# Half of the first product of blocks 1 and 2 as Strassen steps, with weight quarters combined on GpSimd

## The chip, the cores and the metric

The kernel runs on one core of one Trainium2 chip. The metric is the device time of one execution in microseconds. TensorE is called PE, VectorE DVE, ScalarE ACT, GpSimd POOL and SyncE SP; "PEld" is PE's loading of weights, which overlaps its matmuls.

## The reference

Attention within chunks of 64 tokens, for 8 heads of 64 columns, and behind it a gated two-layer product over 4608 tokens:

```python
scores = (1/8) * q_c @ k_c.T            # each chunk of 64 tokens, each head
x = (softmax(scores) @ v_c)             # laid out as 4608 tokens x 512
h = x @ w_in                            # 512 -> 2048
g = h * clip(h + 3, 0, 6) / 6
out = g @ w_out                         # 2048 -> 512
```

## The kernel before, in words

**Blocks.** The tokens go as 9 blocks of 512 (`NBLK`, L25). Block n has two halves of 4 heads, called heads n0 and n1. For each, `Attention` (L205 to L329) runs scores (PE), maximum, subtraction, exponential, sum, division, a transpose and a product with v on PE, and leaves the half block's x in SBUF, for blocks 0 to 2 as a high and a low part (`keep`, `rest`, L312 to L325). PE's tile `two` is one, so the scores of a half wait for the `rest` of the half before.

**Numbers in two parts.** Every f32 product is three matmuls with 128x128 weights and 512 columns: high by high, high by low, low by high (`passes`, L334 to L338). A high part is a cast on ACT, the low part a subtraction on DVE.

**Block 0** is a plain two-layer product while the weights are still coming in and being converted (16 column groups `ft` of w_in and 16 row groups of w_out, 8 tiles each, called a0 to a7 and b0 to b7).

**Blocks 1 and 2.** Their first product is plain too: for each block all 16 `ft` (`mm`, L618), 4 x 3 matmuls each (`mm1_half`, L340), then `relu` (ACT) and `gate` (DVE) into the b tiles (L701 to L714). Their second product is a Strassen product: 7 half-size products in place of 8 (`second_product`, L896).

**Blocks 3 to 8** go in three pairs. The pair is one 2x2 problem and both of its products take seven half-size products per group of columns. In `first_product` (L797) that is, for each of 8 groups p, f1, f5, f6, f7, f2, f3, f4 (`ORDER_A`), 6 matmuls each, and on DVE the sums u2, u4, s7, s3, s4 and four gates (L835 to L851); f2, f3 and f4 accumulate into a bank of an earlier one after its sum was taken, so f3 waits for u4 and f4 for s7. On POOL two subtractions of gates, t1 and t2 (L853, L855). For blocks 1 and 2 t1 and t2 are on DVE (L867, L869).

**Weight sums.** Strassen's products need sums of the quarters of w_in and w_out. For each of 8 groups of either weight (`sum_steps`, L418) `whole` makes a full copy, on DVE (L433) or by a transfer (L430); `combine` (L435 to L438) makes four sums of 128x256 in place, on DVE; `high` and `lower` split them (L443, L446) into one of two `hl` tiles; `send` and `send_own` write them to DRAM (L451, L457), from where the later products fetch them. The groups u = 0 to 7 are of w_out, 8 to 15 of w_in (L755 to L766).

**Slots.** The second product of blocks 1 and 2 needs space: 8 slots, the tiles a0 to a7 of w_in, of which 3 take fetched weights and 5 the split operands (`next_slot`, L489; casts and subtractions L884, L887). Before, slot k is free once the plain product of block 2 with ft 2k+1 is done (L501).

**Order.** All steps are handed to `Schedule` (L52), which knows an engine, a fixed cost, predecessors and a due time for each, and writes one order per engine. Each engine then runs its list in order; a waiting step holds up all behind it on its engine. The cost table is fixed in the code and does not know of two engines getting in each other's way. `PLACES` (L600) names the PE steps behind which a half block's last product, merged with the scores of the next half, is put.

Of the kernel before, what the change touches and what calls it, by code (L numbers as in the profile page):

```python
# [18 lines left out]
P = 128  # L19
# [12 lines left out]
NFP = NFT // 2  # L32
ORDER_A = (1, 5, 6, 7, 2, 3, 4)
# [6 lines left out]
ROWS = []  # L40
# [8 lines left out]
SECOND = STEP * 33  # L49
# [70 lines left out]
def tile_kernel(ctx: ExitStack, tc: tile.TileContext, qk_in, v_in, weights, out):  # L120
# [7 lines left out]
    raw = pool("raw", NDP)  # L128
# [9 lines left out]
    xp = std.enter_context(tc.tile_pool(name="xp", bufs=NDP))  # L138
# [66 lines left out]
    class Attention:  # L205
# [106 lines left out]
        def keep(self):  # L312
            if self.n >= NHI:
                if self.n not in xraw:
                    xraw[self.n] = raw.tile([P, NDP, 2, NT], F32, name="x")
# [101 lines left out]

    def sum_steps(m, p):  # L418
# [16 lines left out]
        def combine():  # L435
            for to, x, y, op in ((q(1, 1), q(1, 0), q(1, 1), ALU.add), (q(1, 0), q(0, 0), q(1, 0), ALU.subtract),
                                 (q(0, 0), q(1, 1), q(0, 0), ALU.subtract), (q(0, 1), q(0, 1), q(0, 0), ALU.subtract)):
                DVE.tensor_tensor(out=to, in0=x, in1=y, op=op)  # L438

        def high():  # L440
            t["hl"] = hp.tile([P, 2, 2, 2, 256], F32R, name="hl")
            t["s"] = t["a"].rearrange("p f (k t) -> p f k t", k=2)
            ACT.copy(out=t["hl"][:, :, :, 0], in_=t["s"])  # L443
# [45 lines left out]
    def next_slot(s, name, until, stream=False):  # L489

        if s == 0:
            first, n = (0, RING) if stream else (RING, NFP - RING)
            k = first + slots[stream] % n
# [8 lines left out]
        return k, before  # L502

# [31 lines left out]


# [4 lines left out]
    spare = {"qk01": lambda: xp.tile([P, 2, NB, 2 * CH], F32, name="x"),  # L541
# [6 lines left out]
    def attention(u, due, scores=(), less=(), keep=(), bank=None):  # L548
# [10 lines left out]
        if u in ROWS:  # L559
            rows = [("negate", "DVE", 0.12, a.negate, ()), *[(f"exp{k}_", "ACT", 2.3, lambda k=k: a.exps(k, e() if k == 0 else None), less if k == 0 else ()) for k in range(4)],  # L560
                    ("invert", "DVE", 0.45, a.invert, ())]
        steps = [("scores", "PE", 1.30, a.scores, ["qk" + u, *scores]), ("max", "DVE", 1.23, a.largest, ()), *rows, ("share", "DVE", 1.22, a.share, ()), ("turn", "PE", 1.07, a.turn, ()),
                 ("turned", "ACT", 1.02, a.turned, ()), ("product", "PE", 2.26 if after else 1.50, products if after else a.product,
                  ["v" + u, *(["qk" + after, *[x for _ in HALF for x in work.take(*RINGS[bank], "product" + u, [made[u]])]] if after else [])]),
# [28 lines left out]
    due_of = {"10": 13 * STEP, "11": 15 * STEP, "20": 20.5 * STEP, "21": 24 * STEP}  # L593
    for s in range(1, NSUP):
        n = NSTD + 2 * s
        for k, u in enumerate((f"{n}0", f"{n + 1}0", f"{n + 1}1", f"{n}1")):
            chain.append(u)
            due_of[u] = STEP * (28, 35.5, 39.3, 42)[k] if s == 1 else START[s - 1] + PART * (30, 51, 73, 94)[k]
    prior = dict(zip(chain[1:], chain))
    PLACES = {"21": ("a", NFT + 14), "30": ("a", NFT + 22), "40": ("s", 0, 1), "41": ("s", 0, 3), "31": ("s", 0, 6)}  # L600
# [21 lines left out]
    def place(u, bank=None):  # L622
        n = int(u[0])
        s = (n - NSTD) // 2
        free = () if n == 1 else [f"b{NFT - 1}"] if n == 2 else [f"b{2 * NFT - 1}"] if s == 1 else [f"x{s - 1}.{i}l" for i in ORDER_A]
        attention(u, due_of[u], [made[prior[u]]] if u != "10" else ["b0"], ["product" + prior[u]], free, bank)
# [74 lines left out]
    for j, (n, ft) in enumerate(mm):  # L701
        first, second, relu, gate, high, lower, sums, send, bank, under = tile_steps(n, ft)
        of = lambda name, back: f"{name}{j - back}" if j >= back else None
        at = STEP * j if n == 0 else STEP * (NFT + 1) + STEP / 2 * (j - NFT)
        apart = j < APART
        before = [] if apart and j % 2 else [of("b", 1)]
        work.add(f"a{j}", "PE", PART * 2 / 3 if apart else PART, [f"{'high' if apart else 'lower'}a{ft // 2}" if n == 0 else None, *before, made[f"{n}0"], *work.take("o" if spare_bank(j) else "h", 4 if spare_bank(j) else 2, f"a{j}", [f"gate{j}"])], first, due=at)
        if apart:
            work.add(f"l{j}", "PE", PART / 3, [f"a{j}", f"lowera{ft // 2}"], under, due=at)
        work.add(f"b{j}", "PE", PART, [f"l{j}" if apart else f"a{j}", of("b", 1), made[f"{n}1"]], second, due=at + PART)  # L710
        if n:
            place_at(("a", j), bank_o)
            add_relu_gate(f"{j}", f"b{j}", bank, lambda n=n, ft=ft: gate_of(ft // NFP, n - 1, ft % NFP), at + STEP, [f"{s}{ft // 2 * 2 % d + k}" for s, d in (("own", NFP), ("c", NFT), *([] if in_dram(1, ft // 2 * 2 % NFP) else [("whole", NFP)])) for k in range(2)])
# [83 lines left out]
    def first_product(s):  # L797
        work.add(f"lay{s}", "none", 0.0, [f"ul{s - 1}.{i}.{k}" for i in ORDER_B for k in range(NFP // 2)], lambda: None)
        before = f"s{s - 1}.{SLOTS - 1}"
        g = GRAIN[s]  # L800
        ceil = lambda n: (n + g - 1) // g
        for p in range(NFP):
            t = {}
            gq = lambda r, c, p=p: gate_of(r, c, p)
            id_ = lambda name, p=p: f"{name}{s}.{p}"
            feeds = [add_fetch(s) for _ in range(ceil(4) + ceil(3))]
            for k, i in enumerate(ORDER_A):
                name = id_(f"f{i}.")
# [25 lines left out]
                new = lambda key, t=t: lambda: keep_tile(t, key, lambda: tp.tile([P, NT], F32, name=key))  # L834
                if i == 1:  # L835
                    work.add(id_("p1."), "ACT", 0.59, [name, f"lay{s}", *work.take("p1", 2, id_("p1."), [id_("u2.")])],
                             lambda o=new("p1"), x=of(1): ACT.copy(out=o(), in_=x()), due=due)
                elif i == 6:
                    work.add(id_("u2."), "DVE", 0.69, [name, id_("p1."), *work.take("u2", 2, id_("u2."), [id_("s3."), id_("s4.")])],
                             add(new("u2"), of(6), of("p1")), due=due)  # L840
                    work.add(id_("u4."), "DVE", 0.69, [id_("f5."), id_("u2."), *work.take("u4", 2, id_("u4."), [id_("s7.")])],
                             add(new("u4"), of(5), of("u2")), due=due)
                elif i == 7:
                    work.add(id_("s7."), "DVE", 0.69, [name, id_("u4.")], add(of(6), of(7), of("u4")), due=due)
                    add_relu_gate(id_("7."), id_("s7."), of(6), lambda f=gq: f(1, 1), due)
                elif i == 2:
                    add_relu_gate(id_("2."), name, of(1), lambda f=gq: f(0, 0), due)
                elif i in (3, 4):
                    out = (lambda f=gq: f(0, 1)) if i == 3 else (lambda f=gq: f(1, 0))
                    work.add(id_(f"s{i}."), "DVE", 0.69, [name, id_("u2.")], add(of(j), of(j), of("u2")), due=due)  # L850
                    add_relu_gate(id_(f"{i}."), id_(f"s{i}."), of(j), out, due)  # L851
                    if i == 3:
# [43 lines left out]
    def second_product(s):  # L896
# [15 lines left out]
        before = f"f{ORDER_A[-1]}.{s}.{NFP - 1}" if s else f"b{len(mm) - 1}"  # L912
# [114 lines left out]
```

## Time and profile before

| | |
|---|---|
| median of 3 runs | 786.94 us (786.46 to 787.82) |
| span of the profiled execution | 784.5 us |
| PE busy | 776.5 us (99%) |
| DVE busy | 634.5 us (81%) |
| ACT busy | 377.4 us (48%) |
| POOL busy | 71.4 us (9%) |
| granted PE clock | 0.999 of full speed |

The span is what the profiler saw from the first to the last instruction. The profiled execution's own time is not among the three runs listed; the median lies 2.44 us above its span, which is what lies around it. Busy shares of engines that overlap do not add up; what matters is which of them something waits for, stretch by stretch.

The stretches by their borders in the trace: block 0 until about 146 us, mixed with block 1 from about 101 us; block 2's plain product 167 to 213.5 us; second product of blocks 1 and 2 213.5 to 299.2 us; then the pairs.

### The profile page before, as it was taken

What the parts mean: (1) busy time and instruction counts of PE and PEld (TensorE: products, weight loads), DVE (VectorE), ACT (ScalarE), POOL (GpSimd) and SP (SyncE); (2) the same over time, 40 slices, a digit from 0 to 9 for tenths busy, and PEclk for the clock granted to TensorE, in tenths of its full rate; (3) what the DMA queues carried; (4) which work ended last, traced back from release to release, by engine and by line L of the source; (5) the groups of instructions that cost most, each with busy time, mean ns of one, the idle gap of its engine ahead of it and who ended that gap; (6) DMA issues with size and microseconds to landing.
All of it is one profiled execution on the core that took longest, in us unless ns stands there. A gap on an engine that the chain in (4) does not pass through costs nothing.

```text
span 784.5 us, 13920 instructions
## 1 busy us (share of the span) xinstructions
PE 776.5 (99%) x5625; PEld 639.6 (82%) x5627; DVE 634.5 (81%) x780; ACT 377.4 (48%) x461; POOL 71.4 (9%) x55
## 2 busy tenths in 40 slices
PE   7999999999999999999999999999999999999998
PEld 4788888888888888888888888888888888888887
DVE  6998998898899988968998687678988657679841
ACT  4998743445554454344644433436543423355330
POOL 0000000000000001322200003231100013222000
PEclk9999999999999999999999999999999999999999
DMA  9999996879779696556676785577666665666572
GB/s 370 408 412 329 353 370 228 280 257 331 288 237 343 215 364 224 195 187 248 203 251 239 248 278 196 197 246 245 197 200 218 217 200 195 202 199 207 197 236 90
DMA packets 69424, 198.05 MB, mean 252 GB/s; under 512 B 7024, under 2 KB 19568, under 8 KB 65008
## 3 DMA queue, kind: packets, MB, share of 16 engines
q1 hardware_dynamic: 69216, 197.03, 72.7%
q8 instruction: 44, 0.72, 0.4%
q14 instruction: 20, 0.16, 0.1%
q10 hardware_dynamic: 144, 0.13, 0.0%
HBM read 153.09 MB, written 44.04 MB: 251 GB/s over the span
## 4 chain that ended last, share of the span: by engine, by line
PE 97%; DMA 1%; DVE 1%; ACT 0%; issue 0%; SPq 0%; ACTq 0%
PE acc L336 22%; PE acc L338 21%; PE acc L337 21%; PE h L336 9%; PE h L338 9%; PE h L337 9%; PE two L228 2%; PE two L278 2%; PE h L304 1%; DMA x<-qk_in 1%; PE two L304 1%; PE acc L304 0%; PE h L352 0%; DVE z L246 0%; DVE m L235 0%; DVE e L266 0%
## 5 line engine op out<-in xcount | busy, mean ns | idle before, releaser
L336 PE MATMUL acc<-wa,ws 128*128 128x512 f32 (+1 forms) x536 | 209.2, 390 | 0.0
L338 PE MATMUL acc<-wa,ws 128*128 128x512 f32 (+1 forms) x536 | 207.8, 388 | 0.0
L337 PE MATMUL acc<-wa,ws 128*128 128x512 f32 (+1 forms) x536 | 207.8, 388 | 0.0
L884 ACT CAST wa<-wb 128x1024 fp32r<-128x1024 f32 x96 | 100.4, 1052 | 110.4 <-PE acc L338 66.2
L887 DVE TENSOR_TENSOR wa<-wb,wa 128x1024 fp32r<-128x1024 f32 x96 | 124.0, 1300 | 26.1 <-ACT wa L884 25.4
L336 PEld LDWEIGHTS acc<-wa,ws 128*128 128x128 f32 x536 | 100.6, 188 | 20.7 <-DVE u L789 0.3
L338 PEld LDWEIGHTS acc<-wa,ws 128*128 128x128 f32 x536 | 100.6, 188 | 20.7
L337 PEld LDWEIGHTS acc<-wa,ws 128*128 128x128 f32 x536 | 100.7, 188 | 20.1
L853 POOL TENSOR_TENSOR wb<-wb 128x512 f32<-128x512 f32 x24 | 31.9, 1330 | 637.6 <-DVE wb L682 624.2
L679 ACT ACTIVATE r<-acc,half 128x512 f32<-128x512 f32 x86 | 58.4, 685 | 51.1 <-DVE acc L789 34.0
L679 ACT ACTIVATE r<-h,half 128x512 f32<-128x512 f32 x42 | 28.9, 688 | 108.8 <-DVE h L789 89.8
L682 DVE SCALAR_TENSOR_TENSOR wb<-r,acc 128x512 f32<-128x512 f32 x86 | 58.0, 679 | 8.4 <-ACT r L679 8.2
L338 PE MATMUL h<-wa,ws 128*128 128x512 f32 (+1 forms) x144 | 55.2, 383 | 0.0
L337 PE MATMUL h<-wa,ws 128*128 128x512 f32 (+1 forms) x144 | 55.2, 383 | 0.0
L336 PE MATMUL h<-wa,ws 128*128 128x512 f32 (+1 forms) x144 | 55.2, 383 | 0.0
L336 PE MATMUL h<-x,wa 128*128 128x512 f32 x132 | 52.2, 396 | 0.0
L338 PE MATMUL h<-x,wa 128*128 128x512 f32 x132 | 51.5, 390 | 0.0
L337 PE MATMUL h<-x,wa 128*128 128x512 f32 x132 | 51.4, 390 | 0.0
L789 DVE TENSOR_TENSOR u<-h,p 128x512 f32<-128x512 f32 x32 | 21.9, 688 | 27.7 <-PE h L338 27.5
L789 DVE TENSOR_TENSOR acc<-acc,u 128x512 f32<-128x512 f32 x48 | 32.8, 695 | 9.6 <-PE acc L338 9.6
L682 DVE SCALAR_TENSOR_TENSOR wb<-r,h 128x512 f32<-128x512 f32 x42 | 28.6, 682 | 14.1 <-ACT r L679 14.0
L855 POOL TENSOR_TENSOR g<-wb,wb 128x512 f32<-128x512 f32 x24 | 38.7, 1613 | 1.9
(116 smaller groups left out, 1299.0 us busy)
## 6 DMA issues: line engine op xcount, KB each, us to landing
ws<-b SPq DMA_DIRECT2D x84, 512.0 KB, 4.6
ws<-a SPq DMA_DIRECT2D x72, 512.0 KB, 4.2
qk<-qk_in SPq DMA_DIRECT2D x17, 1024.0 KB, 7.5
wa<-b SPq DMA_DIRECT2D x28, 512.0 KB, 6.3
a<-wa SPq DMA_DIRECT2D x40, 256.0 KB, 6.1
v<-v_in SPq DMA_DIRECT2D x17, 512.0 KB, 5.4
wa<-w_in_out SPq DMA_DIRECT2D x8, 1024.0 KB, 12.2
wb<-w_in_out SPq DMA_DIRECT2D x8, 1024.0 KB, 11.2
```

Source lines behind the costliest of these rows:

```text
L228: PE.matmul(self.s[o, a, c, :], lhsT=self.qk[rows, 0, c, o], rhs=self.qk[rows, 1, c, o], start=True, stop=True)
L278: PE.transpose(out=self.tp[:, a, i], in_=self.e[:, a, 2 * i:2 * i + 2].rearrange("p c t -> p (c t)"), identity=ident)
L336: PE.matmul(ps, lhsT=a_h, rhs=b_h, start=first, stop=False, skip_group_check=more)
L337: PE.matmul(ps, lhsT=a_h, rhs=b_l, start=False, stop=False, skip_group_check=more)
L338: PE.matmul(ps, lhsT=a_l, rhs=b_h, start=False, stop=last, skip_group_check=more)
L679: ACT.activation(out=t["r"], in_=ps(), func=AF.Relu, bias=half, scale=1.0 / 6.0)
L682: work.add("gate" + name, "DVE", 0.69, ["relu" + name, *more], lambda: DVE.scalar_tensor_tensor(out=out(), in0=t["r"], scalar=1.0, in1=ps( ...
L789: return lambda: DVE.tensor_tensor(out=out(), in0=x(), in1=y(), op=ALU.add)
L853: work.add(id_("t1."), "POOL", 1.45, [id_("gate3."), id_("gate2.")], lambda f=gq: POOL.tensor_tensor(out=f(0, 1), in0=f(0, 1), in1=f(0, 0) ...
L855: work.add(id_("t2."), "POOL", 1.45, [id_("t1."), id_("gate7.")], lambda f=gq, p=p: POOL.tensor_tensor(out=t2_of(p), in0=f(1, 1), in1=f(0, ...
L884: ACT.copy(out=g_ops[s, i, pp][:, :, 0], in_=src())
L887: work.add(low, "DVE", 1.22, [high], lambda i=i, pp=pp, src=src: DVE.tensor_tensor(out=g_ops[s, i, pp][:, :, 1], in0=src(), in1=g_ops[s, i ...
```

## The change

Of the 16 `ft` of blocks 1 and 2's plain first product, 8 stay plain (0, 1, 8, 9, 2, 3, 10, 11, which are p = 0 to 3). The other 8 (p = 4 to 7) go through `first_product(0)`: seven half-size products for each p. They take the sums of w_in from the `hl` tiles in SBUF (`parked`) and the plain quarters from the a tiles, so nothing is fetched for them. Sums and splits of x are new steps (`first_x_steps`): two taken from the attention's PSUM banks and one more on DVE, four on POOL, four casts on ACT, four subtractions on DVE; they use the last row groups of w_out's tiles (b3, b7) and the tiles a0, a4, a1, a5. All 16 `combine` go to POOL, and so do t1 and t2 of blocks 1 and 2. The sums of w_in for p = 4 to 7 come ahead of those for p = 0 to 3, which move into the second product's stretch. Slots are freed by the new products. The halves 40 and 41 take their exponentials as 16 pieces on ACT, with sums, instead of one exponential on ACT and a subtraction and a sum on DVE. Block 2's attention is due four steps of 5.448 us earlier; blocks 3 and 4's halves go in the order 30, 31, 40, 41. Buffers for x are renamed (not shown).

```diff
+NPL = 4
+PLAIN = [p + q + NFP * r for p in range(0, NPL, 2) for r in range(2) for q in range(2)]
+FIRST = {0: list(range(NFT)), 1: PLAIN, 2: PLAIN}
+HELD = {5: 0, 6: 4, 7: 1, 4: 5}
...
-ROWS = []
+ROWS = ["40", "41"]
+XDVE = ["x0.s0c"]
...
-SECOND = STEP * 33
+SECOND = STEP * (17 + 2 * NPL) + PART * 7 * (NFP - NPL)
+STEPS = SECOND - PART * 7 * (NFP - NPL)
+COMBS = [u for u in range(16)]
...
-        def combine():
+        def combine(engine):
...
-                DVE.tensor_tensor(out=to, in0=x, in1=y, op=op)
+                engine.tensor_tensor(out=to, in0=x, in1=y, op=op)
...
-            before = [f"b{2 * NFT + 2 * k + 1}", *[f"{step}{NFP + (2 * k + q) % NFP}" for step in ("own",) for q in range(2)]]
+            before = [f"f4.0.{2 * (k % 4) + 1}", *owns(k)]
...
+        work.add("x0.s0", "DVE", 1.22, ["product20", "rest10", "c7", "own6", "own7"], from_banks("20", 5, x(1, 0, 0)), due=due_of["20"])
+        work.add("x0.s1", "DVE", 1.38, ["product21", "x0.s0c"], from_banks("21", 6, of(5)), due=due_of["21"])
...
+            on = name not in XDVE
+            work.add(name, "POOL" if on else "DVE", 2.7 if on else 1.22, after, op(POOL if on else DVE, i, one, two, kind))
...
+            work.add(f"x0.{i}h", "ACT", 1.05, [last, f"b{2 * NFT + 2 * k + 1}", *owns(k)], lambda i=i: high(i))
+            work.add(f"x0.{i}l", "DVE", 1.22, [f"x0.{i}h"], lambda i=i: lower(i))
...
+        if i in (1, 2, 4):
+            return w_of(0, p + NFP * (i == 4))[:, :, 256 * (i != 1):256 * (i != 1) + 256]
+        row, col = {5: (1, 1), 7: (1, 0), 6: (0, 0), 3: (0, 1)}[i]
+        return parked[0, p][:, row, col]
...
-    PLACES = {"21": ("a", NFT + 14), "30": ("a", NFT + 22), "40": ("s", 0, 1), "41": ("s", 0, 3), "31": ("s", 0, 6)}
+    PLACES = {"21": ("a", NFT + 10), "30": ("f", 0, 4), "31": ("s", 0, 0), "40": ("s", 0, 2), "41": ("s", 0, 4)}
...
-    mm = [(n, ft) for n in range(NHI) for ft in range(NFT)]
+    mm = [(n, ft) for n in range(NHI) for ft in FIRST[n]]
...
-    for u in range(2 * NFP):
+    for u in [*range(NFP), *range(NFP + NPL, 2 * NFP), *range(NFP, NFP + NPL)]:
...
-        due = SECOND + (4 * (u - 7) if u < NFP else -35 + 5.5 * (u - 8))
+        due = STEPS - 8 + 4 * (u - 7) if u < NFP else STEPS - 3 + PART * 7 * (p - NPL) if p >= NPL else SECOND + 10 + 12 * p
+        last = [f"f3.0.{p}"] if u >= NFP + NPL else []
...
-        work.add(f"comb{u}", "DVE", 1.70, [f"whole{u}"], combine)
-        work.add(f"top{u}", "ACT", 1.05, [f"comb{u}", *work.take("hl", 2, f"top{u}", [f"send{u}"])], high)
+        work.add(f"comb{u}", *(("POOL", 3.2, [f"whole{u}"], lambda f=combine: f(POOL)) if u in COMBS else ("DVE", 1.70, [f"whole{u}"], lambda f=combine: f(DVE))))
+        work.add(f"top{u}", "ACT", 1.05, [f"comb{u}", *work.take("hl", 2, f"top{u}", [f"send{u}", *last])], high)
...
+    SLOT_OF = (2, 0, 5, 6, 4, 1, 3, 7)
...
-        for p in range(NFP):
+        for p in range(0 if s else NPL, NFP):
...
-                work.add(f"t1.0.{p}", "DVE", 0.69, [f"gate{2 * NFT + p}", f"gate{NFT + p}"], lambda p=p: DVE.tensor_tensor(
+                work.add(f"t1.0.{p}", "POOL", 1.45, gates, lambda p=p: POOL.tensor_tensor(
...
+    first_x_steps()
+    first_product(0)
     add_units(0)
     second_product(0)
```

## Rows read from the trace of the kernel before

**Rows 1.** The page: busy time, share, instructions; chain that ended last, by engine.
```profile
PE 776.5 (99%) x5625; PEld 639.6 (82%) x5627; DVE 634.5 (81%) x780; ACT 377.4 (48%) x461; POOL 71.4 (9%) x55
...
PE 97%; DMA 1%; DVE 1%; ACT 0%; issue 0%; SPq 0%; ACTq 0%
```

**Rows 2.** Waits of PE, the longest: tile, line, releaser: us, times, longest.
```profile
PE h L154 <- DVE half L142: 0.9, 1, 0.9
```

**Rows 3.** Timeline of PE: start, us, engine, line, operation.
```profile
208.02 0.39 PE L336 MATMUL h<-x,wa 128*128 128x512 f32 x1
...
213.46 0.39 PE L336 MATMUL acc<-wa,wa 128*128 128x512 f32 x1
...
299.21 0.39 PE L336 MATMUL acc<-wa,ws 128*128 128x512 f32 x1
```

**Rows 4.** Windows: stretch, its length, busy us of PE, PEld, DVE, ACT, POOL.
```profile
20.00:100.80 80.80, 80.55 (x629) 65.88 (x622) 74.66 (x89) 69.79 (x82) 0.00 (x0) 1.00 1.01 376
100.80:146.00 45.20, 45.20 (x321) 37.23 (x320) 40.05 (x67) 18.81 (x25) 0.00 (x0) 1.00 0.78 271
146.00:167.00 21.00, 21.00 (x274) 17.36 (x273) 19.60 (x30) 9.48 (x13) 0.00 (x0) 1.00 0.80 275
167.00:213.50 46.50, 46.50 (x329) 38.59 (x328) 39.87 (x61) 23.41 (x30) 0.00 (x0) 1.00 0.92 328
213.50:299.20 85.70, 85.70 (x745) 71.27 (x744) 79.18 (x88) 43.24 (x47) 0.00 (x0) 1.00 0.82 285
299.20:386.00 86.80, 86.80 (x510) 71.95 (x509) 70.96 (x95) 39.60 (x56) 24.12 (x16) 1.00 0.61 205
```

**Rows 5.** Groups of instructions, whole run: count, busy us, mean ns, idle before.
```profile
L438 DVE TENSOR_TENSOR a<-a 128x256 f32<-128x256 f32 x64 | 27.0, 424 | 3.7 <-DMA a<-wa 1.5 <-DMA a<-wb 0.6
...
L789 DVE TENSOR_TENSOR u<-acc,u 128x512 f32<-128x512 f32 x32 | 22.0, 690 | 1.0
...
L446 DVE TENSOR_TENSOR hl<-a,hl 128x1024 fp32r<-128x1024 f32 x16 | 19.4, 1220 | 1.0 <-ACT hl L443 1.0
...
L837 ACT COPY p<-acc 128x512 f32<-128x512 f32 x24 | 13.9, 580 | 6.8 <-PE acc L338 6.8
...
L867 DVE TENSOR_TENSOR wb<-wb 128x512 f32<-128x512 f32 x8 | 5.4, 684 | 0.0
...
L145 ACT ACTIVATE warm<-half 128x1 f32<-128x1 f32 x1 | 0.2, 203 | 0.0
```

**Rows 6.** Groups of DVE, 213.5 to 299.2 us.
```profile
L887 DVE TENSOR_TENSOR wa<-wb,wa 128x1024 fp32r<-128x1024 f32 x20 | 24.2, 1214 | 3.4 <-ACT wa L884 3.0
...
L438 DVE TENSOR_TENSOR a<-a 128x256 f32<-128x256 f32 x8 | 3.4, 423 | 0.2
```

**Rows 7.** Timeline of POOL, then of DVE, 320 to 324 us.
```profile
320.18 1.29 POOL L853 TENSOR_TENSOR wb<-wb 128x512 f32<-128x512 f32 x1 [6.82 <-DVE wb L682]
321.54 2.16 POOL L855 TENSOR_TENSOR g<-wb,wb 128x512 f32<-128x512 f32 x1
...
320.61 1.93 DVE L266 TENSOR_TENSOR e<-e,z 128x1024 f32<-128x1024 f32 x1
322.60 0.69 DVE L789 TENSOR_TENSOR u<-h,p 128x512 f32<-128x512 f32 x1
```

**Rows 8.** Groups of DVE, 299.2 to 386 us, a stretch with POOL work.
```profile
L887 DVE TENSOR_TENSOR wa<-wb,wa 128x1024 fp32r<-128x1024 f32 x6 | 10.0, 1680 | 0.7 <-ACT wa L884 0.7
...
L266 DVE TENSOR_TENSOR e<-e,z 128x1024 f32<-128x1024 f32 x2 | 3.9, 1935 | 0.0
```

**Rows 9.** Timeline of DVE and PE: attention of halves 11, 20 and 21.
```profile
99.61 1.21 DVE L325 TENSOR_TENSOR x<-two,x 128x1024 fp32r<-128x1024 f32 x1
...
129.72 1.09 PE two L228 x64
...
165.24 1.28 DVE L325 TENSOR_TENSOR x<-acc,x 128x512 fp32r<-128x512 f32 x2
```

**Rows 10.** DMA issues: count, KB each, median us to landing.
```profile
wa<-b SPq DMA_DIRECT2D x28, 512.0 KB, 6.3
```

More of the change, by code (lines that the diff above doesn't have):

```diff
@@ L492, in next_slot @@
             first, n = (0, RING) if stream else (RING, NFP - RING)
-            k = first + slots[stream] % n
+            k = SLOT_OF[first + slots[stream] % n]
         else:
@@ L559, in attention @@
         if u in ROWS:
-            rows = [("negate", "DVE", 0.12, a.negate, ()), *[(f"exp{k}_", "ACT", 2.3, lambda k=k: a.exps(k, e() if k == 0 else None), less if k == 0 else ()) for k in range(4)],
+            rows = [("negate", "DVE", 0.12, a.negate, ()), *[(f"exp{k}_", "ACT", 1.15, lambda k=k: a.exps(k, e() if k == 0 else None), less if k == 0 else ()) for k in range(8)],
                     ("invert", "DVE", 0.45, a.invert, ())]
@@ L563, in attention @@
                  ("turned", "ACT", 1.02, a.turned, ()), ("product", "PE", 2.26 if after else 1.50, products if after else a.product,
-                  ["v" + u, *(["qk" + after, *[x for _ in HALF for x in work.take(*RINGS[bank], "product" + u, [made[u]])]] if after else [])]),
+                  ["v" + u, *(["qk" + after, *[x for _ in HALF for x in work.take(*RINGS[bank], "product" + u, [made[u], *alike.get(u, [])])]] if after else [])]),
                  ("keep", "ACT", 1.24 if after else 1.03, a.keep, keep)]
@@ L624, in place @@
         s = (n - NSTD) // 2
-        free = () if n == 1 else [f"b{NFT - 1}"] if n == 2 else [f"b{2 * NFT - 1}"] if s == 1 else [f"x{s - 1}.{i}l" for i in ORDER_A]
-        attention(u, due_of[u], [made[prior[u]]] if u != "10" else ["b0"], ["product" + prior[u]], free, bank)
+        free = () if n == 1 else [f"b{NFT - 1}"] if n == 2 else [f"b{2 * NFT + PLAIN[-1]}"] if n == 3 else [f"f1.0.{NFP - 1}", "x0.s2b"] if n == 4 else [f"x{s - 1}.{i}l" for i in ORDER_A]
+        attention(u, due_of[u], [made[prior[u]], *alike.get(prior[u], [])] if u != "10" else ["b0"], ["product" + prior[u]], free, bank)
     RINGS = {}
@@ L797, in first_product @@
     def first_product(s):
-        work.add(f"lay{s}", "none", 0.0, [f"ul{s - 1}.{i}.{k}" for i in ORDER_B for k in range(NFP // 2)], lambda: None)
-        before = f"s{s - 1}.{SLOTS - 1}"
+        work.add(f"lay{s}", "none", 0.0, [f"ul{s - 1}.{i}.{k}" for i in ORDER_B for k in range(NFP // 2)] if s else [f"out{et}" for et in range(NET)], lambda: None)
+        before = f"s{s - 1}.{SLOTS - 1}" if s else f"b{2 * NFT + PLAIN[-1]}"
         g = GRAIN[s]
         ceil = lambda n: (n + g - 1) // g
-        for p in range(NFP):
+        laid = {}
+        for p in range(0 if s else NPL, NFP):
             t = {}
+            more = lambda r, p=p: [] if s else left(p + NFP * r)
             gq = lambda r, c, p=p: gate_of(r, c, p)
             id_ = lambda name, p=p: f"{name}{s}.{p}"
-            feeds = [add_fetch(s) for _ in range(ceil(4) + ceil(3))]
+            feeds = [add_fetch(s) for _ in range(ceil(4) + ceil(3))] if s else []
             for k, i in enumerate(ORDER_A):
@@ L809, in first_product @@
                 j = {2: 1, 3: 5, 4: 7}.get(i, i)
-                feed, until = feeds[ceil(4) * (k // 4) + k % 4 // g]
-                over = k % 4 % g == g - 1 or k == 6
-                after = [before, feed, f"x{s}.{i}l"]
+                feed, until = feeds[ceil(4) * (k // 4) + k % 4 // g] if s else (None if i in (1, 2, 4) else f"less{NFP + p}s", [])
+                over = s and (k % 4 % g == g - 1 or k == 6)
+                after = [before, feed, f"x{s}.{i}l" if s or i in HELD else None]
                 if i == j:
@@ L816, in first_product, with product @@
                     after.append(id_({2: "p1.", 3: "u4.", 4: "s7."}[i]))
-                def product(i=i, j=j, k=k, t=t, over=over):
-                    w = ahead[0][:, k % 4 % g]
+                def product(i=i, j=j, k=k, t=t, over=over, p=p):
+                    w = ahead[0][:, k % 4 % g] if s else weight_of(p, i)
                     ps = t[j] if i != j else keep_tile(t, i, lambda: bank(i))
@@ L850, in first_product @@
                     work.add(id_(f"s{i}."), "DVE", 0.69, [name, id_("u2.")], add(of(j), of(j), of("u2")), due=due)
[L851 to L852 removed]
+                    add_relu_gate(id_(f"{i}."), id_(f"s{i}."), of(j), out, due, more(int(i == 4)))
+                    if i == 3 and s:
                         work.add(id_("t1."), "POOL", 1.45, [id_("gate3."), id_("gate2.")], lambda f=gq: POOL.tensor_tensor(
@@ L910, in send @@
             return f
-        before = f"f{ORDER_A[-1]}.{s}.{NFP - 1}" if s else f"b{len(mm) - 1}"
+        before = f"f{ORDER_A[-1]}.{s}.{NFP - 1}"
         g = GRAIN[s]
@@ L978, in tile_kernel @@
     for s in range(1, NSUP):
-        first = [u for u in chain if (int(u[0]) - NSTD) // 2 == s and int(u[0]) >= NHI]
+        n = NSTD + 2 * s
+        first = [f"{n}0", f"{n + 1}0", f"{n + 1}1", f"{n}1"]
         for name, engine, cost, after, f, reads in x_steps(s):
```

113 lines of the change are left out of this document (82 added, 31 removed).

## The prediction

> **What bounds the kernel now.** I read the page first: PE is busy 99% of the span, and the chain that ended last is PE for 97% [rows 1]. Then PE's waits: there are seven, the longest 0.9 us [rows 2], and the windows show where they are not: from 100.8 us on PE is busy for all of every stretch, at a granted clock of 1.00, that is at 2.4 GHz [rows 4]. A busy PE need not be at its peak, so I took the spacing from PE's timeline: 24 matmuls of 512 columns from 208.02 to 213.46 us, 5.44 us or 226.7 ns each [rows 3]. They follow one another at that pace, so a matmul that is left out is worth 0.227 us as long as nothing else comes last. What could come last is DVE. It is 81% busy on average, but by stretch: 40.05 of 45.2 us, 19.60 of 21.0, 39.87 of 46.5 and 79.18 of 85.7, and 70.96 of 86.8 in the first pair's first product [rows 4]. The change works on the first four of these.
>
> **PE.** Removed: 8 of 16 column groups in each of two blocks, 12 matmuls each, 16 x 12 = 192. Added: 4 groups p of seven products of 6 matmuls, 4 x 7 x 6 = 168. Net 24 matmuls fewer, 24 x 0.2267 = 5.44 us [rows 3]. Shape and operand types are the same. All of it is on the path. The median of the runs stands 2.44 us above the profiled span (786.94 against 784.5), and I take that to stay: without any new wait the time is 786.94 - 5.44 = 781.5 us. What remains is whether the new stretches keep PE fed.
>
> **DVE before the border of 213.5 us** (208.1 after). From 100.8 us on it is busy 40.05 + 19.60 + 39.87 = 99.5 of 112.7 us [rows 4]. Out: the quarter sums, 64 less the 8 that lie behind the border, 56 x 0.424 = 23.7 [rows 5, 6]; six of eight t1, 6 x 0.684 = 4.1 [rows 5]; one low part of the weight sums, 1.2 [rows 5]; about two operand splits that get their slots later, 2.4 [rows 6]. In: five sums for each of 4 groups p, of which one p's fall behind the border, 15 x 0.69 = 10.4; two subtractions from PSUM banks as four half tiles, 4 x 0.68 = 2.7 (the like of the pair at 165.24) [rows 9]; one more subtraction and four low parts, 5 x 1.22 = 6.1 [rows 5]. The gates are as many as before. Net -31.4 + 19.2 = -12.2: 87.3 us of work in 112.7 - 5.4 = 107.3 us, 20 us free.
>
> **POOL**, idle there until now, gets 12 of the 16 quarter sums, t1 and t2 and the four x sums. A 128x512 subtraction takes it 1.29 us [rows 7]. The quarter operations of 128x256 have no row on POOL: at least half of 1.29, 0.65, and at most 1.29; DVE's own sizes stand as 0.424 to 0.684 [rows 5], so I take 0.62 x 1.29 = 0.80, or 3.2 us for one weight group. A 128x1024 x sum is two of 1.29. Before the border: 12 x 3.2 + 8 x 1.29 + 4 x 2.58 = 59 us in 107 us. POOL itself has room; nobody waits on it closely, as the longest chain (x sums 4 x 2.58 = 10.3 us, then a cast and a low part) has from block 2's x to the last f4, some 26 us by the due times of the code.
>
> **The two engines get in each other's way.** In the timeline, DVE's division, which reads two SBUF tiles, starts at 320.61 under a POOL subtraction that runs until 321.47, and takes 1.93 us in place of 1.22; the POOL subtraction that starts at 321.54 takes 2.16 in place of 1.29, until DVE's has ended at 322.54. The DVE sum right behind it, which reads a PSUM bank, takes its usual 0.69 under POOL work [rows 7]. So operations with two SBUF inputs exclude POOL's, others don't. The Trainium skill states this as a rule (page "SBUF — State Buffer", section "Who interferes with whom"): a DVE instruction with two SBUF inputs and a GpSimd one that reads SBUF take turns, whoever is second blocks until the first is done. The trace agrees. By that rule the quarter sums don't leave DVE's time: each POOL operation may block DVE for as long as DVE would have worked itself, and the gain would go.
>
> What it costs, from rows: in the stretch from 299.2 us the splits take 6 x (1.68 - 1.21) = 2.8 us more than undisturbed and the divisions 2 x (1.935 - 1.22) = 1.4 [rows 6, 8]; 4.2 us for 24.12 us of POOL work [rows 4], 0.18 us of DVE per us of POOL. There DVE's operations on two SBUF tiles are few: about 12 of 1.13 us, 16% of the stretch. Before the new border they are about 37 of 107 us, 35% (12 low parts of weights, 12 halves of the full copies, four divisions, the x sums). At the same rate POOL costs DVE 59 x 0.18 = 10.6 us; scaled with the share, 59 x 0.39 = 23 us; below, nothing. Against 20 us free, DVE runs from comfortably to just full.
>
> **Behind the border**, up to 299.2 us, DVE has 79.18 us of work now [rows 4]. Out: 8 quarter operations 3.4 [rows 6], ten t1 and t2 6.8, and for two halves the subtraction and sum that ACT takes over, 2 x 2.3. In: one more low part 1.2, the last p's five sums 3.4, and parts of halves 31 and 50 that now fall in the stretch, 4.9. Net -5.3: 74 of 85.7 us. POOL gets 4 x 3.2 + 8 x 1.29 = 23 us there, under DVE work that is mostly on two SBUF tiles: 4 us at the low rate, some 16 at full exclusion three times in four. That is 78 to 90 us; the split operands are made up to three slots ahead, three times two parts of 1.36 us, 8 us, which covers most of the excess.
>
> **Edits that I cost at nothing.** ACT's exponentials in 16 pieces, between 16 x 0.2 and 16 x 0.58 us for each of two halves [rows 5]: at most 9.3 us twice, and ACT is busy 43.24 of 85.7 us there [rows 4]; without that room the halves would come late for the pair that starts at 299 us. Casts of x: four of about 1 us on ACT. Transfers: the sums are still sent, as many bytes; on SP the sends of four w_in groups now stand among the fetches of the second product. A fetch takes 6.3 us to land [rows 10] and each of three fetch slots is refilled eight parts of 1.36 us ahead, 10.9 us; a send that waits for a late low part holds the fetches behind it, and 4.6 us of that is covered.
>
> **The sum.** 5.44 us off, and a new wait of PE between 0 and some 10 us (below nothing is excluded: nothing else of PE's work goes). The nearest row is the stretch from 299.2 us, where PE stays busy throughout although POOL blocks DVE [rows 4, 8]; but DVE is emptier there, so I take 1.0 us, one or two such blocks that outlast f3's 1.3 us of slack (two parts of 1.36 less two sums of 0.69). Forecast: 781.5 + 1.0 = **782.5 us**.
>
> **Rivals.**
> First, the slower side: **the shared way into SBUF fills DVE before the border.** If POOL's 59 us take not 0.18 or 0.39 but 0.5 of their time out of DVE, that is 29.5 us against 20 free; PE waits 9.5 us for gates, sums or low parts, and the time is 781.5 + 9.5 = 791.0. It is slower from (20 + 5.44 + 1.57) / 59 = 0.46 on. For it: the shares above, and a fixed order on DVE that puts a blocked operation ahead of u2 or u4. Against it: POOL loses the turn as often as DVE (2.16 for 1.29), and 0.46 is above the scaled rate. The rule of the Trainium skill's page "SBUF — State Buffer" ("Who interferes with whom"), taken for every POOL operation, is this rival at its full price; the rows so far bear out a part of it.
>
> Second, **a late start of the second product.** Before, slots 3 to 6 came free 22 to 5 us ahead of the border; now slot 6 comes 19 us ahead, 4 and 1 some 5 and 4, 3 and 7 at the border (by the parts of 1.36 us in the code), while DVE also has the last p's nine operations, 6.2 us. The second to fourth splits are due 2.7, 5.4 and 8.2 us behind it; if they queue behind those nine, about 3 us are lost: 784.5. Against it: ACT and DVE need only 2.3 us for one split.
>
> Third, **block 2 comes late.** Its plain product starts 8 x 2.72 = 21.8 us earlier, at about 146 us. Now the low part of half 11's x, which frees the tile `two`, begins at 99.61 us, the scores of half 20 at 129.72 and the low part of 21 ends at 166.5 [rows 9]: 36.8 us for two halves, which could end at 137.6 when begun at once, 8.4 us in time. But from 20 to 100.8 us DVE is busy 74.66 of 80.8 us [rows 4]; were it to begin 13 us later, behind weight copies, PE would stand for 5 us: 786.5.
>
> **Chances.** Forecast 0.47 (781 to 784, all faster). First rival 0.22, of which 0.02 ends without a difference. Second 0.15, of which 0.12 faster, 0.03 the same. Third 0.10: 0.02 faster, 0.08 the same. The rest, 0.06, is several small waits: 0.01 faster, 0.02 the same, 0.03 slower. A measurement of this kernel can tell 0.2%, 1.57 us, from no change. Together: faster 0.62, same 0.15, slower 0.23. The range goes from 781.0, the sum without waits less half a us of the runs' spread, over the second and third rival and into the first, to 789.0; by the cases this leaves out 0.03 below and 0.17 above.
>
> **What would show it.** Right: 24 matmuls fewer, PE busy without a break from 30 us to the end, the border at about 208 us and the next at 294, span about 780. DVE's low parts and divisions longer than 1.22 us under POOL's quarter sums, by 10 to 23 us in all before the border. Wrong: a wait of PE for DVE's u or s sums (first rival), for splits right behind the border (second), for block 2's x at about 146 us (third), or quarter operations far from 0.80 us.

## The result: slower, and the profile after

The changed kernel takes 792.92 us (median of 4 runs, 791.19 to 793.87) against 786.7 us for the kernel before (4 runs, 786.32 to 787.82): a ratio of 1.0069 with a 95% interval of 1.0052 to 1.0087. The forecast was 782.5 us, in a range from 781.0 to 789.0. The profiled execution has a span of 790.3 us against 784.5.

The page's busy times, the answer to [rows 1], and the group of the quarter operations, now on POOL, the answer to [rows 5] (columns as there):

```profile
PE 775.2 (98%) x5603; PEld 635.6 (80%) x5603; DVE 634.1 (80%) x726; ACT 388.6 (49%) x531; POOL 174.9 (22%) x139
...
PE 83%; DVE 6%; DMA 3%; POOL 3%; ACT 2%; issue 1%; SPq 1%; DVEq 0%; POOLq 0%; ACTq 0%
...
L447 POOL TENSOR_TENSOR a<-a 128x256 f32<-128x256 f32 x64 | 67.0, 1049 | 165.5 <-DMA b<-wb 111.0
```

PE's share of the chain that ended last fell from 97% to 83%. POOL's busy time grew by 103.5 us, of which the 64 quarter operations are 67.0: 1.049 us each on average. DVE's busy time is the same to half a us although 38 us of its own work went to POOL and a few us to ACT, while some 20 us were added: the rest, about 20 us over the whole run, is longer operations.

PE's waits down to half a us, the answer to [rows 2] (those of 0.6 to 0.8 us left out):

```profile
PE acc L343 <- DVE wb L752: 3.0, 1, 3.0
PE two L235 <- issue: 2.7, 1, 2.7
PE h L161 <- DVE half L149: 0.9, 1, 0.9
PE acc L343 <- DVE g L864: 0.9, 1, 0.9
...
PE acc L343 <- DMA wa<-b: 0.5, 1, 0.5
```

New are the waits of 3.0 and 2.7 us and that for `g` (L864), which lie before the border between the first and the second product, and the last one, behind it. The same stretches by windows (columns as in [rows 4]):

```profile
100.00:125.00 25.00, 22.28 (x219) 18.08 (x219) 20.08 (x26) 9.19 (x13) 9.51 (x11) 1.00 0.97 329
125.00:150.00 25.00, 24.67 (x230) 19.98 (x228) 23.13 (x27) 11.24 (x15) 14.69 (x14) 1.00 0.73 248
150.00:175.00 25.00, 24.84 (x107) 19.93 (x107) 20.52 (x18) 11.45 (x15) 22.68 (x17) 1.00 0.90 301
175.00:200.00 25.00, 20.99 (x206) 16.80 (x206) 21.32 (x28) 12.41 (x18) 21.51 (x19) 0.93 0.61 222
```

PE idles here, and it is not DVE that is full (20 to 23 of 25 us): from 150 us on it is POOL, 22.68 and 21.51. How POOL reaches PE is read from three timelines of the same stretch. POOL:

```profile
161.61 2.41 POOL L565 TENSOR_TENSOR wb<-wb,xb 128x1024 f32<-128x1024 f32 x1
163.99 4.96 POOL L447 TENSOR_TENSOR a<-a 128x256 f32<-128x256 f32 x4
168.91 2.39 POOL L565 TENSOR_TENSOR wb<-xc,wb 128x1024 f32<-128x1024 f32 x1
171.38 3.26 POOL L565 TENSOR_TENSOR wb<-wb,xc 128x1024 f32<-128x1024 f32 x1
174.60 5.86 POOL L447 TENSOR_TENSOR a<-a 128x256 f32<-128x256 f32 x4
```

DVE:

```profile
167.46 0.67 DVE L752 SCALAR_TENSOR_TENSOR wb<-r,h 128x512 f32<-128x512 f32 x1
170.07 2.31 DVE L455 TENSOR_TENSOR hl<-a,hl 128x1024 fp32r<-128x1024 f32 x1 [1.94 <-ACT hl L452]
172.31 3.41 DVE L273 TENSOR_TENSOR e<-e,z 128x1024 f32<-128x1024 f32 x1
175.64 1.74 DVE L572 TENSOR_TENSOR wa<-wb,wa 128x1024 fp32r<-128x1024 f32 x1
177.31 0.68 DVE L752 SCALAR_TENSOR_TENSOR wb<-r,acc 128x512 f32<-128x512 f32 x1
```

PE:

```profile
174.62 0.39 PE L345 MATMUL h<-wa,hl 128*128 128x512 f32 x1
178.04 0.50 PE L343 MATMUL acc<-wa,hl 128*128 128x512 f32 x1 [3.03 <-DVE wb L752]
178.37 0.49 PE L344 MATMUL acc<-wa,hl 128*128 128x512 f32 x1
178.66 0.63 PE L345 MATMUL acc<-wa,hl 128*128 128x512 f32 x1
179.09 0.63 PE L343 MATMUL acc<-wa,hl 128*128 128x512 f32 x1
```

The four quarter operations of one weight group, from 163.99 us, take 4.96 us in place of four times 0.74. ACT's cast of that sum begins when they end, at 168.99, and DVE stands 1.94 us before the low part L455, as its list is fixed. Then come three operations that read two SBUF tiles, under two x sums (L565) and the next quarter operations on POOL: 2.31, 3.41 and 1.74 us in place of 1.22 each. The gate behind them (L752), which reads a PSUM bank and is not blocked itself, comes at 177.31, and PE gets the bank for its next product at 178.04. This gap of 3.4 us between two matmuls costs more than itself: the matmuls from 178.66 on start 0.43 us apart in place of 0.227, and the granted clock of the window is 0.93. Those spacings are PE's two levels, 1.2 and 2.4 GHz.

The wait of 2.7 us put down to "issue" is at 118.8 to 121.5 us: the scores of half 21 need the tile `two`, and x0.s0 (L561), which now also reads it, began on DVE at 120.19, behind a low part that had waited 0.80 us for ACT and POOL. The wait for `g` is at 183.5 us. DVE, then PE:

```profile
117.65 1.49 DVE L455 TENSOR_TENSOR hl<-a,hl 128x1024 fp32r<-128x1024 f32 x1 [0.80 <-ACT hl L452]
120.19 1.21 DVE L561 TENSOR_TENSOR wb<-two,xb 128x1024 f32<-128x1024 f32 x1
...
118.39 0.39 PE L345 MATMUL h<-xc,wa 128*128 128x512 f32 x1
121.50 1.16 PE L235 MATMUL two<-qk 64*64 64x64 f32 x64 [2.72 <-issue]
122.93 0.39 PE L344 MATMUL h<-xb,wa 128*128 128x512 f32 x1
123.16 0.39 PE L345 MATMUL h<-xb,wa 128*128 128x512 f32 x1
184.43 0.50 PE L343 MATMUL acc<-xd,hl 128*128 128x512 f32 x1 [0.91 <-DVE g L864]
```

The border came at 218.45 us (the last first-product group's f4 starts at 217.09, six matmuls) against 213.46 [rows 3] and the 208.1 predicted; the next border at 304.77 against 299.21. The second product took 86.3 us against 85.75. So practically all of the loss is ahead of the border.

### The profile page after: what moved, and what is told of

Same layout as the page of the kernel before. It is cut to its first block, busy times and chain, and to the rows that moved or that the text cites. A ratio compares the mean times of both kernels' runs of the same rounds, so it can differ in the third digit from the quotient of the medians.

```text
span 790.3 us, 14001 instructions
## 1 busy us (share of the span) xinstructions
PE 775.2 (98%) x5603; PEld 635.6 (80%) x5603; DVE 634.1 (80%) x726; ACT 388.6 (49%) x531; POOL 174.9 (22%) x139
## 4 chain that ended last, share of the span: by engine, by line
PE 83%; DVE 6%; DMA 3%; POOL 3%; ACT 2%; issue 1%; SPq 1%; DVEq 0%; POOLq 0%; ACTq 0%
PE acc L343 19%; PE acc L344 19%; PE acc L345 19%; PE h L343 7%; PE h L345 7%; PE h L344 7%; POOL a L447 2%; PE two L235 2%; PE two L285 2%; DVE hl L455 1%; PE h L311 1%; DVE a L442 1%; DMA wa<-b 1%; DMA a<-wa 1%; DMA b<-wb 1%
## 5 line engine op out<-in xcount | busy, mean ns | idle before, releaser
L974 DVE TENSOR_TENSOR wa<-wb,wa 128x1024 fp32r<-128x1024 f32 x96 | 128.6, 1349 | 30.3 <-ACT wa L971 29.8
L447 POOL TENSOR_TENSOR a<-a 128x256 f32<-128x256 f32 x64 | 67.0, 1049 | 165.5 <-DMA b<-wb 111.0
L749 ACT ACTIVATE r<-acc,half 128x512 f32<-128x512 f32 x90 | 61.2, 686 | 39.9 <-DVE acc L864 36.6
L749 ACT ACTIVATE r<-h,half 128x512 f32<-128x512 f32 x38 | 26.1, 687 | 103.4 <-DVE h L864 98.4
L752 DVE SCALAR_TENSOR_TENSOR wb<-r,acc 128x512 f32<-128x512 f32 x90 | 60.8, 680 | 7.9 <-ACT r L749 7.9
L864 DVE TENSOR_TENSOR u<-h,p 128x512 f32<-128x512 f32 x32 | 22.0, 689 | 27.3 <-PE h L345 27.1
L864 DVE TENSOR_TENSOR acc<-acc,u 128x512 f32<-128x512 f32 x48 | 33.0, 696 | 9.8 <-PE acc L345 9.7
L752 DVE SCALAR_TENSOR_TENSOR wb<-r,h 128x512 f32<-128x512 f32 x38 | 25.9, 682 | 12.9 <-ACT r L749 12.9
L343 PE MATMUL acc<-wa,wa 128*128 128x512 f32 x88 | 34.9, 397 | 0.5 <-DMA wa<-b 0.5
L345 PE MATMUL acc<-wa,wa 128*128 128x512 f32 x88 | 34.3, 390 | 0.0
```

The lines of the kernel that those rows point to most:

```text
L343: PE.matmul(ps, lhsT=a_h, rhs=b_h, start=first, stop=False, skip_group_check=more)
L345: PE.matmul(ps, lhsT=a_l, rhs=b_h, start=False, stop=last, skip_group_check=more)
L447: engine.tensor_tensor(out=to, in0=x, in1=y, op=op)
L749: ACT.activation(out=t["r"], in_=ps(), func=AF.Relu, bias=half, scale=1.0 / 6.0)
L752: work.add("gate" + name, "DVE", 0.69, ["relu" + name, *more], lambda: DVE.scalar_tensor_tensor(out=out(), in0=t["r"], scalar=1.0, in1=ps( ...
L864: return lambda: DVE.tensor_tensor(out=out(), in0=x(), in1=y(), op=ALU.add)
```

## The experiments

Theory A, formed from these rows: GpSimd's queue and its turn-taking with VectorE make the low parts of the weight sums late, and lists in a fixed order stand behind them. Rivals: B, the new order is too tight in itself; C, VectorE is simply full. The runs are called e1 to e12.

**Without the quarter sums (e1).** They are left out, so that the weight sums are not formed; every other engine keeps its order.

```diff
-            for to, x, y, op in ((q(1, 1), q(1, 0), q(1, 1), ALU.add), (q(1, 0), q(0, 0), q(1, 0), ALU.subtract),
+            for to, x, y, op in () and ((q(1, 1), q(1, 0), q(1, 1), ALU.add), (q(1, 0), q(0, 0), q(1, 0), ALU.subtract),
...
```

> The 64 quarter operations on GpSimd are left out (the weight sums are then not formed), the written order of every other engine stays. Theory A (GpSimd's queue and its taking turns with VectorE hold up the low parts of the weight sums, and VectorE's list stands behind them): all of the waits go, about 24 matmuls fewer, 781 to 783 us. Theory B (the new order itself is too tight: block 2's attention earlier, the chain through the x sums, the slots): the waits stay for the most part, 788 to 793 us. Between 783 and 788 both have a share.

781.5 us (ratio 0.9923, 0.9909 to 0.9938). PE has no wait over 0.9 us left, and the borders are where they were predicted, at 208.2 and 293.8 us:

```profile
PE h L161 <- DVE half L149: 0.9, 1, 0.9
PE two L285 <- DVE e L273: 0.8, 1, 0.8
```

This shows two things. The 24 matmuls are worth what the sum said, 781.5 us; that it agrees to the tenth is luck, as single runs go from 780.7 to 782.6. And block 2's earlier attention, the x sums, the slots and the fetches cost nothing by themselves: theory B falls. Matched by their order with this run's, the changed kernel's matmuls fall back by 2.8 us at 118 to 123 us, by 5.0 us at 175 to 182 us and by 1.2 us at 184 us; this is 9.0 of the some 10.7 us lost from 100 us to the border.

**The quarter sums on VectorE (e2).**

```diff
-COMBS = [u for u in range(16)]
+COMBS = []
```

> All 16 quarter sums back on VectorE (27 us of its time), everything else as changed; the order is planned anew. Theory A: GpSimd has room, no turns are lost to quarter sums, 781 to 786 us. Theory C (VectorE has no room for them once the half Strassen product is on it): VectorE full before the border, 793 to 800 us. Theory B: near 790 us.

804.98 us (1.0217, 1.0200 to 1.0233). In this placement VectorE is full, 24.76 of 25 us (windows, columns as in [rows 4]):

```profile
150.00:175.00 25.00, 18.70 (x80) 14.49 (x78) 24.76 (x25) 9.28 (x12) 13.64 (x7) 1.00 0.53 176
```

and the longest of PE's waits is for the cast of a weight sum:

```profile
PE acc L343 <- ACT hl L452: 13.7, 1, 13.7
```

So theory C is true of VectorE with this work on it, and theory A's 781 to 786 us was wrong here: the move to GpSimd does pay against leaving the sums where they were, by 12 us, once the Strassen steps are in. It is not enough.

**The x sums on VectorE (e3).**

```diff
-XDVE = ["x0.s0c"]
+XDVE = ["x0.s0c", "x0.s2", "x0.s2b", "x0.s3", "x0.s3b"]
```

> The four sums of x that were put on GpSimd go to VectorE (4 x 1.2 us), the quarter sums stay on GpSimd. Theory A: GpSimd loses 10 us of its busiest stretch (about 157 to 195 us) and the 3.2 us wait for f7 there goes, 787 to 790 us. Theory B or C: no gain, 791 to 796 us.

794.15 us (1.0096, 1.0071 to 1.0122): no gain. Of the wait of 3.0 us 0.8 us is left, and one of 6.1 us for another bank came.

**The cost in the plan (e4).**

```diff
-        work.add(f"comb{u}", *(("POOL", 3.2, [f"whole{u}"], lambda f=combine: f(POOL)) if u in COMBS else ("DVE", 1.70, [f"whole{u}"], lambda f=combine: f(DVE))))
+        work.add(f"comb{u}", *(("POOL", 4.2, [f"whole{u}"], lambda f=combine: f(POOL)) if u in COMBS else ("DVE", 1.70, [f"whole{u}"], lambda f=combine: f(DVE))))
```

> Same work on the same engines; only the planner's cost of a quarter sum on GpSimd is 4.2 us, as measured, in place of 3.2. If the wrong cost in the fixed order is what makes engines stand behind late steps: 784 to 789 us. If it is the load itself: within 2 us of 793.

787.89 us (1.0016, 1.0001 to 1.0032; single runs from 786.79 to 792.14). With the same work on the same engines, another order is worth some 4 to 5 us (5.0 by the medians, 4.2 by the two ratios). The rest, 6.4 us to the run without quarter sums, stays.

**GpSimd busy, but reading nothing (e5).** This separates the two halves of theory A, a slow GpSimd and two engines that take turns. The weight sums are again not formed.

```diff
-                engine.tensor_tensor(out=to, in0=x, in1=y, op=op)
+                engine.memset(t["a"].rearrange("p f t -> p (f t)")[:, :768], 0.0)
```

> Each quarter sum on GpSimd becomes a memset of 768 columns, an instruction of about the same length (0.74 us by its rate in the trace of before) that reads nothing; the weight sums are then not formed. GpSimd's list, its waits and those of all others stay as written. Theory A1 (the two engines taking turns is what costs: VectorE's operations blocked, GpSimd's stretched from 0.74 to 1.05 us): 781 to 784 us. Theory A2 (GpSimd is too slow and too late even when it runs undisturbed, 3.0 us for four): 787 to 793 us.

781.6 us (0.9925, 0.9905 to 0.9944). The stand-ins take 0.742 us each, as long as an undisturbed quarter operation (median 0.744). The group, of the whole execution:

```profile
L447 POOL MEMSET a<- 128x768 f32 x64 | 47.4, 742 | 172.3 <-DVE a L442 120.3 <-DMA a<-wa 38.0 <-DVE wb L752 5.1
```

From 125 to 175 us GpSimd is about as busy as after the change, from 175 to 200 us less (14.53 us in place of 21.51); the first two stretches (windows, columns as in [rows 4]):

```profile
125.00:150.00 25.00, 25.00 (x234) 20.83 (x233) 20.25 (x28) 11.28 (x16) 13.40 (x17) 1.00 0.89 301
150.00:175.00 25.00, 24.75 (x115) 20.37 (x113) 24.75 (x24) 13.07 (x17) 22.95 (x22) 1.00 0.82 286
```

GpSimd 22.95 of 25 us, VectorE 24.75, and PE hardly waits. GpSimd, then VectorE, in this stretch:

```profile
164.03 3.26 POOL L565 TENSOR_TENSOR wb<-wb,xc 128x1024 f32<-128x1024 f32 x1
167.22 6.38 POOL L447 MEMSET a<- 128x768 f32 x8
...
164.95 3.41 DVE L273 TENSOR_TENSOR e<-e,z 128x1024 f32<-128x1024 f32 x1
168.29 1.21 DVE L572 TENSOR_TENSOR wa<-wb,wa 128x1024 fp32r<-128x1024 f32 x1
170.62 1.22 DVE L572 TENSOR_TENSOR wa<-wb,wa 128x1024 fp32r<-128x1024 f32 x1
172.35 1.22 DVE L455 TENSOR_TENSOR hl<-a,hl 128x1024 fp32r<-128x1024 f32 x1
```

Under eight stand-ins three operations with two SBUF inputs keep their 1.21 to 1.22 us. The x sums still read, and the division that begins under one takes 3.41 us as after the change, but at no cost to PE. So neither a busy GpSimd nor a busy VectorE costs the time, nor the x sums' reading: the quarter sums' reading SBUF against VectorE does. All 11.3 us between this run and the changed kernel hang on it; no run separates what VectorE loses by it from what the quarter sums lose. That the operations under the stand-ins are not stretched agrees with the Trainium skill, "SBUF — State Buffer", section "Who interferes with whom", which lets a GpSimd instruction that only writes pass a VectorE instruction with two SBUF inputs, and one that reads not.

**The move alone (e6)**, in the kernel before.

```diff
-                DVE.tensor_tensor(out=to, in0=x, in1=y, op=op)
+                POOL.tensor_tensor(out=to, in0=x, in1=y, op=op)
...
-        work.add(f"comb{u}", "DVE", 1.70, [f"whole{u}"], combine)
+        work.add(f"comb{u}", "POOL", 3.2, [f"whole{u}"], combine)
```

> The kernel before with only the quarter sums moved to GpSimd (cost 3.2 in the plan), no Strassen steps in the first product. If the move alone costs by taking turns, 788 to 793 us; if it costs only where the sums of w_in are due inside the first product and GpSimd also has the x sums, 786.5 to 787.5 us as before.

790.05 us (1.0032, 1.0020 to 1.0045). The quarter operations take 0.952 us there. So the move costs some 2 to 3 us even where VectorE had room for the sums. The rest comes only with the Strassen steps; that it is by their deadlines is argued, not shown.

**Parts of the quarter sums on VectorE**, both with 4.2 us in the plan: the first two w_in groups that the first product waits for (e7), and the first three w_out groups (e8).

```diff
-COMBS = [u for u in range(16)]
+COMBS = [u for u in range(16) if u not in (12, 13)]
```

> As e4 (4.2 us in the plan), and the quarter sums of the first two w_in groups that the first product waits for go to VectorE. Theory A: GpSimd loses 8 us in the stretch from 150 to 175 us, where it was busy 24 of 25 us and where e4's last waits are: 782 to 786 us. If VectorE has no room there (as in e2): 789 to 796 us.

796.08 us (1.0108, 1.0081 to 1.0135); VectorE 24.79 of 25 us from 150 to 175 us, PE's longest wait 5.2 us for the cast of a weight sum.

```diff
-COMBS = [u for u in range(16)]
+COMBS = [u for u in range(16) if u not in (0, 1, 2)]
```

> As e4, and the quarter sums of the first three w_out groups go to VectorE, early, where it is less full. Theory A: everything on GpSimd comes up to 12 us sooner, 782 to 786 us. If VectorE is full there too: 788 us or more.

789.39 us (1.0021, 1.0011 to 1.0031). By theory A both were to win, and neither did.

**Four orders more**, all with 4.2 us in the plan. First with the x sums on VectorE (e9), by the edit of `XDVE` shown above:

```diff
-XDVE = ["x0.s0c"]
+XDVE = ["x0.s0c", "x0.s2", "x0.s2b", "x0.s3", "x0.s3b"]
```

> As e4 (4.2 us in the plan) with the four x sums on VectorE. Turn-taking says: GpSimd loses 10 us between 150 and 175 us, VectorE gains 5 us of work there that GpSimd's quarter sums block; 785 to 789 us. If lateness of the w_in sums were all, 782 to 785 us.

785.26 us (0.9979, 0.9964 to 0.9995; single runs from 784.5 to 790.09): the only run that forms the sums and is faster than the kernel before, by 1.7 us, which is just what can be told. Its profiled execution is the one of 790.09 us, so its trace does not show the 785 us.

Then t1 and t2 of blocks 1 and 2 on VectorE (e10):

```diff
-                work.add(f"t1.0.{p}", "POOL", 1.45, gates, lambda p=p: POOL.tensor_tensor(
+                work.add(f"t1.0.{p}", "DVE", 0.69, gates, lambda p=p: DVE.tensor_tensor(
...
-                work.add(f"t2.0.{p}", "POOL", 1.45, [f"t1.0.{p}", f"gate{2 * NFT + NFP + p}" if p < NPL else f"gate7.0.{p}", *free], lambda p=p: POOL.tensor_tensor(
+                work.add(f"t2.0.{p}", "DVE", 0.69, [f"t1.0.{p}", f"gate{2 * NFT + NFP + p}" if p < NPL else f"gate7.0.{p}", *free], lambda p=p: DVE.tensor_tensor(
```

> As e4 with t1 and t2 of blocks 1 and 2 back on VectorE (16 x 0.6 us there for 16 x 1.3 us and more on GpSimd). Turn-taking says: an operation on VectorE costs 0.6 us for certain, on GpSimd it blocks up to 1.1 us of VectorE's operations on two SBUF tiles; 784 to 788 us. If VectorE has no room: 790 us or more.

791.12 us (1.0053, 1.0034 to 1.0071): the 784 to 788 us that turn-taking alone said did not come.

Then the blocked lengths of two VectorE operations in the plan (e11):

```diff
-        work.add(f"whole{u}", *(("SP", 1.57) if in_dram(m, p) else ("DVE", 1.38)), ["room", *work.take("a", 2, f"whole{u}", [f"less{u}s"])], whole)
+        work.add(f"whole{u}", *(("SP", 1.57) if in_dram(m, p) else ("DVE", 1.9)), ["room", *work.take("a", 2, f"whole{u}", [f"less{u}s"])], whole)
...
-        work.add(f"less{u}s", "DVE", 1.22, [f"top{u}"], lower, due=due)
+        work.add(f"less{u}s", "DVE", 1.5, [f"top{u}"], lower, due=due)
```

> As e4, and the plan also has the lengths that the blocked operations on VectorE showed: 1.5 us for the low part of a weight sum, 1.9 us for a full copy. If the remaining waits of e4 are places where the fixed order is still wrong: 783 to 786 us. If the two engines together are simply full from 150 to 175 us: 787 to 791 us, as e4.

791.14 us (1.0043, 1.0026 to 1.0059). Better costs in the plan, and a worse time than with one of them. The plan knows a mean, while the blocking falls where two lists happen to meet; that this is the reason is not shown.

Last, these lengths and the x sums on VectorE together, by the first and the third of these edits (e12):

> As e11 with the x sums on VectorE. If order and turns both count, the better of e9 and e11 less 1 to 2 us: 782 to 786 us. If the stretch is full whatever the order: 786 to 790 us.

790.65 us (1.0036, 1.0023 to 1.0049). The four orders span 6 us, more than the sum promised. One wait is the longest of PE in all four profiled executions, that for the cast of a weight sum (L452): 1.9, 3.1, 3.0 and 2.9 us. So the chain is late in all of them. As the first of them took 790.09 us, these waits do not say why the first order takes 785 us otherwise; no theory here predicted it, and it stays open.

## Why the prediction was wrong

**The PE term** was right: 24 matmuls, 5.44 us, shown by the two runs without reading quarter sums, 781.5 and 781.6 us.

**The step that failed** is the one on POOL: "POOL itself has room; nobody waits on it closely". Its room was worked out from undisturbed lengths, 59 us before the border with quarter operations at 0.80. Undisturbed they are even shorter, 0.744, but on average they took 1.049 as they were blocked too: 4.2 us for a weight group in place of 3.2. From 100 to 200 us POOL was busy 68.4 us and in the last 50 of them 88% of the time. I had seen POOL lose its turn, 2.16 us for 1.29 [rows 7], and used it as an argument against the first rival; it belongs to the loss, which is gone when stand-ins lose no turn (e5). And somebody does wait closely: each weight sum goes whole, quarters, cast, low part, and DVE's fixed list stands at the low part, with gates and bank releases for PE behind it. I followed the x sums and not this chain.

**The new wait** was therefore 1.0 us by the sum and 11.4 by the runs (792.92 less 781.5). It depends on the fixed order too: with 4.2 us in the plan it is 6.4 (e4). The prediction had no term for this.

**The DVE terms** held in size. What the blocking took from DVE between 100 and 212 us, in the four groups that it stretched most, is 12 x (1.594 - 1.22) for low parts, 12 x (0.943 - 0.684) for the halves of the full copies, 4 x (1.776 - 1.22) for divisions and 4 x (1.383 - 1.22) for the x low parts: 4.5 + 3.1 + 2.2 + 0.7 = 10.5 us, about the low end of the 10.6 to 23 predicted. The groups:

```profile
L455 DVE TENSOR_TENSOR hl<-a,hl 128x1024 fp32r<-128x1024 f32 x12 | 19.1, 1594 | 7.4 <-ACT hl L452 7.3
L442 DVE TENSOR_TENSOR a<-wb 128x512 f32<-128x512 f32 x12 | 10.8, 943 | 3.3 <-DMA wb<-u 3.3
L273 DVE TENSOR_TENSOR e<-e,z 128x1024 f32<-128x1024 f32 x4 | 7.1, 1776 | 0.0
L572 DVE TENSOR_TENSOR wa<-wb,wa 128x1024 fp32r<-128x1024 f32 x4 | 5.5, 1383 | 0.0
```

DVE did not fill up, as the low end said; the column that I had no term for is the last one, 7.3 us in which it waited for the cast of a weight sum. How much of this is the quarter sums' own is read from the same groups of the run with the stand-ins:

```profile
L455 DVE TENSOR_TENSOR hl<-a,hl 128x1024 fp32r<-128x1024 f32 x12 | 17.4, 1446 | 3.1 <-ACT hl L452 3.0
L442 DVE TENSOR_TENSOR a<-wb 128x512 f32<-128x512 f32 x12 | 7.7, 686 | 1.8 <-DMA wb<-u 1.8
L273 DVE TENSOR_TENSOR e<-e,z 128x1024 f32<-128x1024 f32 x4 | 7.1, 1768 | 0.0
L572 DVE TENSOR_TENSOR wa<-wb,wa 128x1024 fp32r<-128x1024 f32 x4 | 4.9, 1214 | 0.0
```

The low parts and the divisions are stretched there too, by the x sums and the other work left on POOL. The difference is 1.7 + 3.1 + 0.0 + 0.6 = 5.4 us of blocking and 4.3 us of waiting for the cast: the lateness of the chain weighs nearly as much as the blocking.

**The first rival** had the resource, the place and nearly the time (791.0) right, and the road wrong: it let DVE run full, and DVE was busy 85 of the 100 us from 100 us on. That its time came near is luck. The chance I gave it, 0.22, was too low; the row on which I chose 1.0 us, the stretch from 299.2 us, has 24 us of POOL in 87 (28%, against 68 of 100 us here), and nothing on DVE that waits for POOL there.

**The other rivals** did not happen as put. No split was late behind the border, and PE's wait for a fetch there is 0.5 us. Block 2's x came in time, the wait at 149 us being 0.3 us; the wait at 118.8 us is part of that chain, but without the quarter sums it is gone.

## What to carry to other kernels

Work that is moved to an engine that takes turns with another at reading SBUF must be priced on both sides and along its chain: what it takes from the other engine, by how much it is stretched itself, and which fixed list stands until it is done. A mean of busy time says little, as PE ran through 99% of a stretch in which VectorE and GpSimd were each busy over 90%, with half of GpSimd's work reading nothing (e5). To tell occupancy from contention, replace the instructions by ones of equal length that read nothing.

## What the runs showed of the hardware that was not expected

GpSimd was stretched more than VectorE. Between 100 and 212 us its quarter operations lost 54 x (1.015 - 0.744) = 14.6 us, against the 5.4 us that VectorE's four groups above lost by them; single ones took up to 1.82 us in the whole run.

```profile
L447 POOL TENSOR_TENSOR a<-a 128x256 f32<-128x256 f32 x54 | 54.7, 1015 | 135.7 <-DMA b<-wb 111.0 <-DVE a L442 9.1 <-DMA a<-wa 4.5
```

PE's wait of 3.0 us, a gap of 3.4 us, was followed by eight matmuls 0.43 us apart, which adds 1.7 us, half of the gap again. The wait of 2.7 us at 118.8 us, a gap of 3.1 us, was followed by the scores and then by matmuls at the usual spacing (122.93, 123.16), and so was the wait of 0.9 us at 183.5 us.
